# One of the first batch's loads in two halves, with a cast for each, and the instruction order written anew around it

## The chip, the core and the metric

The kernel runs on one core of a Trainium2 chip. A core has five engines that each follow their own queue in order: TensorE (PE, matrix products into PSUM), VectorE (DVE), ScalarE (ACT), GpSimd (POOL) and SyncE (SP, which here only starts DMAs). Semaphores tie the queues together. The metric is the time of one execution on the device in microseconds.

## What is computed

The inputs are q, k and v of 8 batches, 8 heads, 576 positions and 64 columns, and four weight matrices. All are float32.

```python
q_s = exp(q) / sum over the 64 columns          # per position
k_s = exp(k) / sum over the 576 positions       # per column
kv  = einsum('bhsd,bhse->bhde', k_s, v)         # 64x64 per head
x   = einsum('bhsd,bhde->bhse', q_s, kv)        # then (4608, 512): heads side by side
a, b = x @ w1, x @ w2                           # (4608, 1024) each
out = ((a * b) @ w3) @ w_out                    # (4608, 512)
```

The reference also takes the maximum off before each exponential, which cancels in the quotient.

## The kernel before

**Products of weights.** `w3 @ w_out` is one 1024x512 matrix, W3O. The kernel makes it once (lines 391 to 427): each of eight row blocks of w3 is loaded (`ld w3 n`, 512 KB), cast to 16 bits (`w3c`), transposed by TensorE (`w3t`, L406), copied out of PSUM (`w3e`), multiplied with the four cast pieces of w_out (`woc`; products `w3m`, L418) and copied out again (`w3v`).

**Attention.** For each batch b and each half i of the heads (lines 467 to 620): the exponentials of k (`ke`, ACT), a cast of v (`vc`), the exponentials of q (`qe`, ACT), row sums (`qr`, DVE), a reciprocal (`qi`), the normalisation (`qn`, L520), transposes (`qt`, on TensorE at L536 with copies `qv` for batches 0 to 3, by DMA for the others), then the products `kv` (L562), their division by the key sums (`kn`, DVE) and `x` (L607) with its copies to the tile xt (`xc`). The names in the lists below add batch, half and piece.

**Feed-forward.** The 4608 rows are taken in eight groups of 512 or 640. Group 0 is computed plainly (L647): `pa0`, `pa1` give x@w1 and `pb0`, `pb1` give x@w2, each product in two halves of the sum; `pac` copies the one out of PSUM and `pm` multiplies. The others use a Winograd scheme with seven products instead of eight on halves of the group (L712, tasks `x1` to `x4`, `w`, `v1`, `v2`): it needs combinations of the weights (`w1c`, `w2c` casts, `wc0` to `wc3`), combinations of xt (`tt1` to `tt4`), copies (`e1` to `e3`) and sums and products (`k1` to `k5`). Last, `s2` (L816) multiplies with W3O, `s2e` scales the result out of PSUM and `so` stores it.

**Buffers.** Every load lands in one of ten tiles `st`. A load into a tile that is in use waits, on SP's queue, until the reader of the old content is done, and everything behind it on that queue waits too. PSUM has eight tiles `ps`.

**The order.** No scheduler runs when the kernel is built. All steps are first recorded as numbered tasks. ORDER (line 18) lists the numbers in the order in which they are emitted, SLOTS (line 107) the tile of each buffer, and ENGS (line 139) the engine of each task that can run on several:

```python
for n in order:
    if isinstance(n, tuple):
        self.fill(self.pools[n[0]][n[1]], n[2])
    elif self.tasks[n].alts:
        self.tasks[n].emit(engs[n])
```

An entry `('ps', slot, n)` emits n matmuls on a blank tile (L985), which compute nothing that is used; here they are called fills.

Of the kernel before, what the change touches and what calls it, by code (L numbers as in the profile page):

```python
# [18 lines left out]
    ('ps', 0, 11), 12, 6, 0, 1, 2, 3, 14, 120, 96, 97, ('ps', 0, 3), 72, 98, 73, 121, ('ps', 0, 2), 74, 68,  # L19
    122, 75, 80, 99, 123, 8, 81, 4, 69, 5, 82, 76, 10, 124, 128, 9, 83, 7, 84, 129, 104, 100, 130, 13, 105,  # L20
    88, 11, 131, 106, 15, 89, 132, 70, 90, 107, 108, 16, 91, 112, 17, 77, 92, 19, 125, 144, 18, 113, 85,
    142, 114, 101, 143, 109, 115, 145, 133, 71, 20, 116, 146, 147, 117, 93, 78, 140, 21, 134, 126, 135, 86,
    127, 79, 110, 136, 94, 111, 137, 102, 95, 150, 152, 22, 162, 103, 148, 164, 118, ('ps', 3, 2), 151,
    154, 163, 138, 149, 153, 139, 168, 171, ('ps', 5, 8), 155, 169, 24, 170, 23, 156, 141, 87, 119, 25,
    172, 157, 173, 165, ('ps', 2, 2), 181, 166, 158, 180, 475, 159, 160, 167, 469, 161, 481, 174, 478, 176,
    175, 472, 182, 484, 466, 183, 487, 467, 26, 479, 468, 188, 488, 470, 473, 184, 471, 190, 485, 482, 486,
    476, 502, 189, 496, 185, 503, 474, 30, 490, 191, 504, 27, 480, 497, 28, 493, 477, 194, 491, 29, 489,
    508, 31, 492, 494, 483, 1382, 495, 1396, 202, 192, 499, 204, 1397, 203, 509, 498, 505, 200, 500, 205,
    511, 510, 501, 506, 214, 1403, 507, 512, 212, 206, 1404, 513, 207, 1389, 196, 215, 1390, 197, 1398,
    213, 1391, 40, 1405, 216, 34, 193, 1392, 217, 1383, 1393, 1399, 208, 1400, 1384, 201, 209, 199, 218,  # L30
    210, 219, 1385, 198, 186, 211, 32, 222, 177, 38, 223, 179, 178, 1386, 33, 220, 224, 1406, 221, 225, 36,
    1407, 226, 229, 232, 227, 230, 1408, 228, 235, 234, 231, 533, 233, 35, 237, 518, 236, 535, 1387, 519,
    563, 514, 534, 520, 37, 515, 548, 539, 42, 516, 549, 517, 522, 521, 564, 537, 552, 536, 538, 554, 523,
    553, 567, 540, 187, 525, 541, 524, 526, 555, 542, 578, 527, 528, 568, 545, 529, 556, 530, 570, 239,
    546, 593, 531, 558, 571, 547, 565, 557, 594, 569, 559, 573, 532, 579, 543, 244, 572, 560, 195, 544,
    597, 595, 574, 598, 575, 566, 246, 582, 550, 561, 608, 583, 596, 600, 623, 551, 601, 584, 576, 624,
    599, 562, 585, 256, 247, 1417, 577, 286, 627, 602, 1410, 245, 586, 242, 605, 609, 603, 240, 606, 1411,
    587, 588, 628, 607, 580, 604, 288, 612, 581, 630, 39, 625, 248, 631, 589, 590, 249, 1409, 613, 610,
    626, 629, 238, 591, 1418, 1388, 611, 614, 41, 615, 632, 1431, 43, 592, 616, 635, 241, 1395, 617, 633,
    618, 636, 254, 1394, 620, 634, 1432, 637, 280, 1402, 621, 1412, 243, 619, 1419, 1401, 622, 255, 1433,  # L40
    284, 252, 281, 257, 1434, 253, 1424, 258, 287, 250, 1435, 259, 1425, 298, 289, 1420, 296, 264, 251,
    265, 1421, 290, 1413, 283, 285, 266, 262, 267, 282, 260, 263, 1426, 291, 261, 44, 271, 268, 272, 273,
    306, 47, 270, 269, 277, 307, 45, 278, 1414, 297, 274, 657, 275, 279, 1427, 640, 308, 276, 294, 309,
    292, 658, 295, 672, 293, 644, 638, 642, 717, 639, 1428, 659, 299, 687, 641, 643, 661, 1430, 663, 673,
    660, 646, 662, 676, 48, 645, 647, 664, 300, 648, 1415, 677, 665, 649, 301, 702, 666, 650, 667, 49, 679,
    703, 668, 669, 1416, 680, 652, 651, 678, 670, 682, 52, 688, 654, 681, 706, 1437, 671, 655, 691, 718,
    302, 683, 707, 1423, 304, 656, 653, 692, 684, 721, 303, 305, 1429, 674, 685, 704, 694, 675, 722, 709,
    705, 693, 695, 686, 689, 724, 696, 732, 690, 725, 697, 699, 733, 698, 723, 708, 710, 700, 727, 711,
    1445, 701, 726, 736, 714, 728, 737, 712, 729, 715, 325, 738, 730, 739, 310, 713, 740, 1446, 716, 312,
    741, 734, 337, 719, 311, 742, 720, 747, 744, 735, 748, 749, 731, 745, 1438, 324, 743, 751, 753, 750,  # L50
    67, 752, 1439, 754, 1440, 755, 1441, 756, 757, 746, 1442, 759, 758, 316, 313, 1444, 317, 319, 314,
    1447, 760, 315, 1436, 320, 766, 321, 781, 318, 767, 1443, 1452, 328, 762, 796, 46, 811, 782, 763, 768,
    335, 761, 1453, 769, 770, 764, 1448, 771, 329, 783, 330, 785, 773, 765, 772, 55, 784, 774, 1454, 812,
    775, 776, 786, 1455, 331, 359, 787, 778, 1456, 1449, 815, 788, 777, 1450, 1466, 789, 779, 1459, 1422,
    797, 790, 816, 798, 780, 54, 800, 323, 332, 791, 799, 1451, 333, 793, 322, 792, 818, 1457, 826, 794,
    819, 1460, 336, 801, 817, 827, 1461, 820, 358, 1462, 795, 338, 821, 50, 803, 813, 334, 822, 804, 830,
    339, 802, 814, 831, 806, 340, 1463, 823, 1467, 805, 1468, 1464, 824, 841, 807, 833, 808, 825, 834,
    1469, 341, 809, 832, 842, 856, 810, 871, 835, 857, 858, 326, 836, 859, 843, 860, 837, 872, 838, 844,
    861, 327, 847, 875, 839, 845, 876, 1473, 846, 828, 1470, 848, 829, 863, 1472, 862, 849, 877, 864, 1465,
    878, 850, 851, 879, 865, 866, 1471, 853, 840, 881, 867, 868, 854, 342, 364, 880, 855, 343, 852, 366,  # L60
    873, 344, 363, 1474, 345, 53, 883, 869, 1475, 1458, 882, 346, 870, 352, 51, 347, 874, 1480, 348, 354,
    1481, 353, 1482, 884, 920, 886, 905, 921, 907, 885, 890, 906, 888, 922, 887, 891, 1483, 908, 1476, 889,
    1484, 894, 924, 1477, 1485, 895, 909, 935, 435, 925, 923, 892, 910, 59, 897, 893, 927, 898, 896, 936,
    912, 928, 362, 899, 926, 913, 911, 929, 900, 930, 914, 950, 60, 901, 902, 951, 915, 931, 939, 62, 917,
    916, 940, 1487, 56, 903, 942, 918, 1486, 904, 954, 943, 941, 955, 937, 944, 932, 373, 945, 938, 957,
    946, 1488, 958, 933, 1489, 365, 934, 952, 947, 367, 349, 355, 919, 1490, 350, 351, 356, 965, 948, 960,
    966, 1494, 953, 357, 995, 374, 969, 996, 1495, 371, 949, 1496, 368, 970, 956, 369, 57, 967, 361, 959,
    1497, 372, 1491, 999, 962, 972, 963, 1515, 973, 961, 980, 971, 968, 370, 981, 1516, 964, 1000, 974,
    975, 1498, 984, 375, 976, 1001, 376, 1002, 1479, 977, 1003, 1508, 978, 982, 1004, 1005, 985, 997, 409,
    1006, 1007, 987, 998, 360, 1501, 377, 1008, 986, 988, 1502, 983, 402, 1503, 1009, 989, 1478, 1504, 979,  # L70
    992, 1500, 1505, 990, 993, 378, 991, 1492, 379, 994, 1493, 1517, 381, 398, 1509, 380, 403, 1510, 382,
    391, 385, 384, 383, 1518, 393, 392, 386, 1014, 387, 1044, 407, 1010, 388, 1511, 389, 390, 66, 1015,
    1029, 1011, 58, 1016, 1030, 1046, 1013, 1017, 1045, 1031, 1018, 1519, 1032, 1059, 1033, 1019, 1035,
    1012, 1034, 1522, 1512, 1047, 1048, 1021, 1513, 1049, 1020, 1022, 1036, 1514, 1523, 1023, 1037, 1050,
    396, 1507, 1038, 1039, 1051, 1040, 64, 1041, 1052, 1524, 1521, 1042, 1060, 1054, 1043, 1026, 1520,
    1053, 1063, 1074, 65, 1055, 1064, 1089, 395, 1525, 408, 1061, 1075, 1066, 1062, 1024, 1067, 1078, 1027,
    1529, 1025, 1079, 1065, 1028, 1090, 1056, 1068, 400, 1069, 1530, 1057, 1526, 1071, 61, 1070, 1081, 394,
    401, 1527, 1093, 1080, 1094, 1091, 1072, 1076, 404, 1531, 1082, 1073, 1092, 1096, 1077, 1095, 405, 410,
    1097, 1104, 1532, 1105, 1083, 1119, 1533, 1098, 1099, 1084, 1120, 1108, 1085, 1101, 1058, 1109, 406,
    1123, 1102, 436, 1086, 1536, 1087, 1103, 1124, 1537, 1100, 399, 1506, 1111, 1088, 1126, 411, 1121,  # L80
    1112, 412, 397, 1550, 1122, 1110, 1127, 1114, 431, 1113, 1543, 1115, 1129, 430, 414, 437, 413, 415,
    1544, 433, 416, 1538, 417, 432, 1499, 1106, 1125, 434, 1107, 1116, 1528, 1551, 1128, 1535, 1552, 1117,
    1130, 1131, 1118, 418, 1132, 450, 419, 451, 1133, 420, 421, 452, 1545, 423, 438, 422, 1546, 453, 1136,
    1553, 1547, 439, 424, 1554, 1168, 425, 1138, 426, 1153, 1556, 1539, 440, 1154, 1134, 63, 1183, 1169,
# [167 lines left out]
def kernel(  # L252
# [11 lines left out]
    nc = tc.nc  # L264
# [754 lines left out]
```

## Time and profile before

| | us |
|---|---|
| median of 4 runs | 234.32 |
| the runs | 233.78, 233.90, 234.75, 235.75 |
| the profiled execution, its own time | 235.75 |
| its span, first to last instruction | 233.9 |
| TensorE busy in the span | 221.0 |
| VectorE busy | 187.7 |
| ScalarE busy | 140.7 |
| GpSimd busy | 91.6 |

The page gives shares of busy time, the span in 40 slices of 5.85 us (each digit is a share in tenths), and the chain of work that ended last. A line of the chain has a start, a length and what ran; "DMA st<-in_v_dram" is time waited for a transfer. In the timeline a line has start, length, engine, source line, operation, tiles written and read, and how often; in brackets stand the engine's idle time just before it and what ended that. L385 is a helper for all casts and copies, so its lines are told apart by their tiles. Matmuls overlap, so TensorE's busy time isn't the time at which it can follow: that is read from the distances between starts.

### The profile page before, as it was taken

The page shows a single profiled execution, that of the slowest core. Times are in us where ns is not written, and L with a number is a line of the kernel's source. Part 1 is how long each engine was busy: PE and PEld are TensorE (multiplying, and loading weights), DVE is VectorE, ACT ScalarE, POOL GpSimd, SP SyncE. Part 2 cuts the span into 40 slices and gives each one's busy share as a digit, 9 for nine tenths or more (in the row PEclk, how much of TensorE's full clock was granted, in tenths as well). Part 3 has the DMA queues.
Part 4 walks back from the last instruction along what each step waited for, and adds up shares of the span by engine and source line. Part 5 has one row for each costly group of instructions (what it writes and reads, how often), then busy time and mean ns, then how long its engine had stood idle before and what let it go on. Part 6 is the DMA issues. An engine that isn't in the chain of part 4 may idle for free.

```text
span 233.9 us, 5571 instructions
## 1 busy us (share of the span) xinstructions
PE 221.0 (94%) x2068; PEld 134.0 (57%) x2068; DVE 187.7 (80%) x457; ACT 140.7 (60%) x306; POOL 91.6 (39%) x81
## 2 busy tenths in 40 slices
PE   7759989998999999999999999999999999999991
PEld 2325444444676558866666676656665866566640
DVE  1322696899899998989998898899988998899930
ACT  2333692483889897768835847576898843525111
POOL 3113344819257787410383444530462503210300
PEclk9999999999999999999999999999999999999998
DMA  6989998788970959938895697859747763041535
GB/s 249 373 311 384 394 387 304 274 334 266 395 299 0 279 188 343 356 122 199 243 236 106 227 299 239 169 146 281 249 85 111 186 125 73 3 90 41 122 91 135
DMA packets 32732, 50.96 MB, mean 218 GB/s; under 512 B 11712, under 2 KB 11712, under 8 KB 32704
## 3 DMA queue, kind: packets, MB, share of 16 engines
q1 hardware_dynamic: 32304, 49.95, 69.5%
q10 hardware_dynamic: 400, 0.66, 1.2%
q8 instruction: 16, 0.26, 0.5%
q14 instruction: 12, 0.10, 0.1%
HBM read 38.80 MB, written 9.44 MB: 206 GB/s over the span
## 4 chain that ended last, share of the span: by engine, by line
PE 78%; DMA 9%; DVE 7%; POOL 2%; ACT 1%; issue 1%; SPq 1%; DVEq 0%; POOLq 0%
PE ps L712 41%; PE ps L816 22%; DMA st<-in_moe_w_dram 6%; PE ps L647 5%; PE ps L418 4%; DMA st<-in_v_dram 3%; PE ps L607 2%; PE ps L562 2%; DVE eq L520 1%; DVE ds L510 1%; DVE ab L664 1%; PE ps L536 1%; POOL eq L520 1%; SPq L332 1%; PE ps L406 1%
## 5 line engine op out<-in xcount | busy, mean ns | idle before, releaser
L736 DVE TENSOR_TENSOR cc<-ps,uu 128x320 f16<-128x320 f32 (+1 forms) x168 | 71.6, 454 | 7.4 <-PE ps L712 3.9
L816 PE MATMUL ps<-W3O,ab 128*128 128x512 f16 x288 | 77.3, 379 | 0.0
L385 ACT COPY uu<-ps 128x320 f32<-128x320 f32 (+1 forms) x144 | 54.1, 406 | 36.3 <-PE ps L712 25.7
L712 PE MATMUL ps<-tt,wc 128*128 128x320 f16 (+1 forms) x336 | 57.5, 288 | 0.1
L712 PEld LDWEIGHTS <-wc 128*128 128x128 f16 x448 | 43.5, 98 | 19.7 <-issue 0.5
L520 POOL TENSOR_TENSOR eq<-eq,ds 128x1152 f16<-128x1152 f16 x14 | 30.0, 2145 | 35.5 <-DVE ds L517 26.9
L712 PEld LDWEIGHTS <-w 128*128 128x128 f16 x336 | 32.1, 98 | 16.6 <-issue 0.8
L712 PE MATMUL ps<-xt,w 128*128 128x320 f16 (+1 forms) x224 | 39.7, 288 | 0.0
L763 POOL TENSOR_TENSOR ab<-cc,cc 128x320 f16<-128x320 f16 (+1 forms) x27 | 20.0, 751 | 47.9 <-DVE cc L736 47.8
L816 PEld LDWEIGHTS <-ab 128*128 128x128 f16 x288 | 27.0, 98 | 18.5 <-issue 0.7
L736 DVE TENSOR_TENSOR ab<-ps,cc 128x320 f16<-128x320 f32 (+1 forms) x56 | 25.1, 454 | 1.4 <-PE ps L712 0.2
L789 ACT ACTIVATE osb<-ps 128x512 f32<-128x512 f32 x29 | 17.2, 602 | 13.9 <-PE ps L816 13.8
L385 ACT CAST xt<-ps 128x512 f16<-128x512 f32 (+3 forms) x43 | 15.0, 408 | 13.8 <-PE ps L607 13.8
L510 DVE TENSOR_REDUCE ds<-eq 128x9 f32<-128x576 f16 x32 | 23.2, 741 | 0.0
L506 ACT ACTIVATE eq<-st 128x576 f16<-128x576 f32 x32 | 21.3, 686 | 2.3 <-DMA st<-in_q_dram 1.8
L712 PE MATMUL ps<-tt,w 128*128 128x320 f16 (+1 forms) x112 | 22.6, 288 | 0.0
L712 PE MATMUL ps<-xt,wc 128*128 128x320 f16 (+1 forms) x112 | 22.3, 288 | 0.0
L475 ACT ACTIVATE ek<-st 128x576 f16<-128x576 f32 x32 | 21.1, 685 | 0.6 <-ACT ek L475 0.6
L689 POOL TENSOR_TENSOR tt<-xt,tt 128x640 f16<-128x640 f16 (+1 forms) x6 | 7.8, 1294 | 22.9 <-DVE tt L689 14.4
L418 PE MATMUL ps<-ab,ab 128*128 128x512 f16 x64 | 15.0, 379 | 0.3 <-DVE ab L385 0.3
L647 PE MATMUL ps<-xt,w 128*128 128x512 f16 x64 | 14.9, 379 | 0.0
L385 POOL CAST v<-st 128x1152 f16<-128x1152 f32 x11 | 13.0, 1193 | 4.3 <-DMA st<-in_v_dram 4.3
(55 smaller groups left out, 199.8 us busy)
## 6 DMA issues: line engine op xcount, KB each, us to landing
st<-in_q_dram SPq DMA_DIRECT2D x16, 576.0 KB, 5.6
st<-in_v_dram SPq DMA_DIRECT2D x16, 576.0 KB, 6.6
st<-in_k_dram SPq DMA_DIRECT2D x16, 576.0 KB, 5.8
out_dram<-osb SPq DMA_DIRECT2D x67, 128.0 KB, 2.6
st<-in_moe_w_dram SPq DMA_DIRECT2D x16, 512.0 KB, 8.5
st<-in_moe_w_out_dram SPq DMA_DIRECT2D x4, 512.0 KB, 7.9
out_dram<-osb ACTq DMA_DIRECT2D x5, 128.0 KB, 2.6
qsT<-eq SPq DMA_TRANSPOSE x8, 3.4
```

The source lines that it names most:

```text
L385: {"DVE": nc.vector.tensor_copy, "POOL": nc.gpsimd.tensor_copy, "ACT": nc.scalar.copy}[eng](out=o, in_=i)
L418: nc.tensor.matmul(pp.tile, lhsT=wT.tile[:, gt * P:(gt + 1) * P], rhs=wo[i][1].tile[:, (gt % 2) * C:(gt % 2 + 1) * C], start=(gt == 0), st ...
L475: nc.scalar.activation(out=ek.tile[:, :, j, :], func=AF.Exp, in_=vk(bk.tile)[:, j].rearrange("p (r d) -> p r d", r=RK))
L506: nc.scalar.activation(out=eq.tile[:, :, j, :], func=AF.Exp, in_=vq(bq.tile)[:, j].rearrange("p (r d) -> p r d", r=RK))
L510: nc.vector.tensor_reduce(out=ds.tile[:, 0, j], axis=AX.X, op=ALU.add, in_=eq.tile[:, :, j, :])
L520: {"POOL": nc.gpsimd, "DVE": nc.vector}[e].tensor_tensor(out=eq.tile, in0=eq.tile, op=ALU.mult, in1=ds.tile[:, 1].rearrange("p j r -> p r ...
L647: nc.tensor.matmul(ps.tile[:, 0:m], lhsT=w[qt][:, ct, fo:fo + P], rhs=x[:, ct, lo:lo + m], start=(ct == 0), stop=(ct == 3))
L712: nc.tensor.matmul(ps.tile[:, 0:h], lhsT=lhs(c), rhs=rhs(c), start=first and c == 0, stop=c == 1, skip_group_check=not first)
L736: return lambda: nc.vector.tensor_tensor(out=dst(), in0=ps.tile[:, 0:h], in1=other.tile[:, 0:h], op=op)
L763: {"POOL": nc.gpsimd, "DVE": nc.vector}[e].tensor_tensor(out=ab.tile[:, 0:h], in0=c11.tile[:, 0:h], in1=c21.tile[:, 0:h], op=ALU.mult)
L789: nc.scalar.activation(out=o(), in_=i(), func=AF.Copy, scale=ISC)
L816: nc.tensor.matmul(po.tile[:, :w], lhsT=rows(ab_buf[(g, ft)].tile), rhs=W3O[:, ft, m * w:(m + 1) * w], start=(ft == 0), stop=(ft == N_FT - 1))
```

## The change

The load of v for batch 0, second half of the heads, becomes two transfers of 288 KB into the two halves of one tile, and its cast becomes two casts of 576 elements per partition, one for each transfer:

```diff
-    JB = []
+    JB = [('v', 0, 1)]
+    XTAIL = []
...
-        if b in JB:
+        if (x, b, i) in JB:
             bb = buf("st")
...
-            if b in JB:
+            if ("v", b, i) in JB:
                 vs = []
                 for j in range(2):
                     def c_j(e, v16=v16, bv=bv, vv=vv, j=j):
                         cast(e, v16.tile[:, :, j, 0:D], vv(bv.tile)[:, j].rearrange("p (r d) -> p r d", r=RK))
                     vs.append(add("POOL", ("vc", b, i, j), c_j, [tv[j]], [bv, v16],
                                   dict(POOL="copy", ACT="sb", DVE="cast"), n=576))
...
+            if b in XTAIL:
+                pieces = [(0, 8)]
```

XTAIL is empty, so nothing of its branch is emitted. The tables ORDER, SLOTS and ENGS are replaced as a whole, so nearly every step stands at another place than before. TensorE's real matmuls are the same in number and shape.

The loads on SP's queue up to the last weight, each with the `st` tile that it lands in:

```text
before: w3 6 [9], w3 3 [0], w3 0 [7], wo 0 [3], w3 1 [1], wo 1 [2], w3 7 [6], w3 4 [1], w3 2 [5], wo 2 [8],
        w3 5 [9], q 0 0 [3], wo 3 [0], v 0 0 [1], k 0 0 [7], q 0 1 [4], k 0 1 [8], v 0 1 [2], then w12 x8
after:  w3 5 [7], w3 3 [4], w3 1 [6], w3 0 [0], w3 6 [3], wo 0 [5], wo 1 [7], w3 7 [8], wo 2 [1], w3 4 [2],
        wo 3 [4], w3 2 [0], q 0 0 [5], q 0 1 [6], k 0 0 [9], v 0 0 [8], w12 x2 [7, 3], k 0 1 [2],
        v 0 1 second half [5], first half [5], w12 x2 [0, 7], w12 [5], w12 x3 [8, 6, 7]
```

What the other engines do first:

```text
ACT  before: woc 0, w3e 6, w3e 1, w3e 7, w3e 2, qe 0 0, woc 3, vc 0 0, w3v 6, ke 0 0, qe 0 1, w3v 3, qe, ke 0 1
     after:  w3c 1, w3c 3, w3e 6, w3c 4, w3e 4, qe 0 0, w3v 7, ke 0 0, w3v 3, w3v 1, qe 0 1, xc 0 0, w2c 0 0, xc 0 0 8, ke 0 1
DVE  before: w3c 3, w3e 3, w3e 0, w3c 1, woc 1, w3c 7, w3c 2, w3e 4, w3e 5, qr 0 0, qi, w3v x4
     after:  w3c 5, w3c 6, w3e 1, w3e 3, w3e 5, w3e 0, woc 1, w3e 7, woc 3, qr 0 0, qi, w3e 2, w3v x3
POOL before: w3c 6, w3c 0, w3c 4, woc 2, w3c 5, qn 0 0, vc 0 1, w1c, w1c, wc0, w2c, wc2, qn 1 0, vc 1 1, wc2
     after:  w3c 0, woc 0, w3c 7, woc 2, w3c 2, qn 0 0, vc 0 0, w1c, qn 0 1, vc 0 1 (second half), wc2, w2c, w1c,
             wc0, wc3, wc1, qn 1 1, vc 1 1
PE   before: fill x11, w3t 3, fill x3, w3t 0, w3t 6, fill x2, w3m 0, ... fills x2, x8, x2 around the first x
     after:  fill x17, w3t 3, w3t 1, w3t 5, w3t 0, w3t 6, fill x3, w3m 1, ... fill x4 after the first x
```

In the new order DVE casts the first half of v 0 1 after two W3O copies and one xt copy.

The number of tasks on each engine that changes, over the whole kernel:

| task | before | after |
|---|---|---|
| fill matmuls | 28 | 24 |
| k5 on DVE, on POOL | 29, 27 | 20, 36 |
| e1, e2, e3 on ACT, on DVE | 144, 24 | 138, 30 |
| tt1 to tt4 on DVE, on POOL | 21, 7 | 16, 12 |
| wc0 to wc3 on DVE, on POOL | 4, 4 | 2, 6 |
| qv on ACT, on DVE | 4, 12 | 9, 7 |
| qn on DVE, on POOL | 2, 14 | 3, 13 |
| pac on ACT, on DVE | 4, 4 | 6, 2 |
| s2e on ACT, on DVE | 29, 7 | 32, 4 |
| w3c on DVE, ACT, POOL | 4, 0, 4 | 2, 3, 3 |
| w3e on DVE, ACT | 4, 4 | 6, 2 |
| xc on ACT, on DVE | 43, 21 | 42, 22 |
| stores issued by SP, by ACT | 67, 5 | 65, 7 |

## The prediction

> **What bounds the kernel now.** I read the page's shares and slices first, then the chain of waits that ended last, then the timeline of the first 40 us.
>
> ```profile
> PE 221.0 (94%) x2068; PEld 134.0 (57%) x2068; DVE 187.7 (80%) x457; ACT 140.7 (60%) x306; POOL 91.6 (39%) x81
> PE   7759989998999999999999999999999999999991
> PEclk9999999999999999999999999999999999999998
> ```
>
> TensorE is full from slice 5 on; the holes are at the start. From the chain (start, length, what):
>
> ```profile
> 2.61 7.99 DMA st<-in_moe_w_dram
> 10.62 0.70 DVE ab L385
> 11.34 5.36 DMA st<-in_moe_w_dram
> 16.76 1.05 POOL ab L385
> ...
> 22.85 6.47 PE ps L418 x30
> ...
> 54.78 2.22 DVE eq L520
> 57.13 0.66 PE ps L536 x9
> ...
> 61.16 10.78 PE ps L712 x78
> ...
> 77.35 7.22 DMA st<-in_v_dram
> 84.69 1.14 POOL v L385
> 85.84 2.11 POOL eq L520
> ...
> 229.10 0.60 ACT osb L789
> ```
>
> Until 17 us weight loads set the pace, then TensorE, with short stops at 57 and 86. L418 x30 in 6.47 us is 0.216 us per 512-column matmul; the 320- and 256-column ones of L712 follow each other at 0.136 and 0.109, transposes at 0.056. With these, all TensorE work without the fills is 206.2 us: 416 x 0.216 + 448 x 0.136 + 336 x 0.109 = 187, the rest transposes, kv and x. I place times by how much of it is done. When `pa1 0 0` starts at 39.55, 23.2 are done: 16.3 lost. At the first Winograd matmul (61.09) 43.0: another 1.7. From there to the end of the last matmul (229) 4.6, then 5.0 of tail. 206.2 + 16.3 + 1.7 + 4.6 + 5.0 is the 233.9 span. Only these losses can change, since the change keeps every real matmul.
>
> Why the 16.3:
>
> ```profile
> 1.19 4.87 PE L985 MATMUL ps<-blank 128*128 128x512 f16 x11 [1.19 <-DVE blank L978]
> 3.72 8.43 SPq L332 DMA_DIRECT2D st<-in_moe_w_dram  x3
> 6.72 0.81 PE L985 MATMUL ps<-blank 128*128 128x512 f16 x3
> 16.76 1.04 POOL L385 CAST ab<-st 128x1024 f16<-128x1024 f32 x1 [7.70 <-DMA st<-in_moe_w_dram]
> 31.14 1.15 POOL L385 CAST v<-st 128x1152 f16<-128x1152 f32 x1 [3.54 <-DMA st<-in_v_dram]
> ```
>
> The SP queue stands for seven us (second line): the eighth load, w3 4, needs the buffer of w3 1, whose cast ends at 11.31. Its data lands at 16.7, 3.5 us after the seventh's 13.2, where busy queues land one every 1.31 (512 KB) or 1.5 us (576 KB). So 2.2 us of transfer time are lost.
>
> **The change, part by part.** *Load order.* Landings by place, from before: 4.1, 5.4, 8.0, 9.3, 10.6, 11.9, 13.2. In the new order the first wait is for the cast of w3 5 (lands 4.1, DVE 0.69: 4.8); the next, wo 3, waits for w3 3, cast on ACT behind w3 1 (8.0 + 2 x 1.05 = 10.0). Six loads are still in flight or queued then, so the queue doesn't dry up: 14.5, 15.8, 17.1, 18.4, 19.7 for the twelve weights (before: 23.6), q at 21.2 and 22.7, k 24.2, v 25.7, two w12 at 27.1 and 28.4, k 29.9, the halved v 31.4, w12 at 32.8 and 34.1.
>
> *W3O.* `w3t 3` can start at 10.05, `w3t 6` after DVE's cast of the fifth load (11.3), four PSUM copies follow on DVE (0.69 each, to 13.9), POOL casts wo 0 by 13.0: the first product at 13.05 (before 10.5). Behind it data is ahead: wo 2's cast is ready at 16.9 and wanted at 17.8, w3 4's 18.2 and 20.0, w3 2's 20.8 and 21.3. TensorE is dense from 13.05, and the last product ends at 29.2 (before 30.8).
>
> *Batch 0.* The first q is in at 21.2; two exponentials (0.68 each, behind an ACT copy to 22.0) end at 23.3, two sums on DVE (0.74) at 24.1, the reciprocal at 24.4, the normalisation on POOL (2.15) at 26.65, and its transposes stand among W3O products, so TensorE doesn't wait. v's cast follows on POOL (1.19, to 27.85), kv at 27.9, the division of both halves on DVE (0.4 each, behind two qsT copies) to 29.3, x at 29.35 (before 31.6). ACT then still owes two W3O copies (0.59) and the second q's exponentials; xt (two of 0.59) is out at 30.9 and w2's cast (1.05) at 32.0; three pb0 pairs (0.43 each) run to 33.3, with about 1.0 of waiting ahead of them. The second q's sums end at 30.7 on DVE, POOL normalises it by 33.2, its transposes end at 34.1, kv at 34.5, division at 35.4, x after it; four pa0/pb0 pairs carry TensorE to 37.5, where the 23.2 are done: **2.05 us earlier**. A POOL cast of w1 at 27.85 that takes 2.05, as at 33.84 before, instead of 1.04 still ends at 29.9, ahead of xt. The split itself: v's cast was 1.15-1.19 in one piece; two halves in parallel are about 0.6 on POOL (33.2 to 33.8) and 0.69 on DVE. It saves 0.5 only if the cast is last; here the transposes end later, so I take 0, bounds -0.5 to +0.4 (one more issue: SP's are 0.37 to 0.45). The DVE half has `kn 0 1`, an xt copy and wc behind it; its data is two us old. The slot passes to the next w12 load when both casts are done (34.0), with all later loads queued behind on SP: it lands at 37.6 (3.6 for a load on an empty queue, as q 1 0's), cast on ACT by 38.9, where the copies of pa1 wait from 39.3: 0.4 of cover, beyond it each us is a us.
>
> *To the Winograd stage.* 19.8 of work. Before lost 0.88 waiting for a normalisation of 2.2 on DVE and 0.8 in x. The new order puts that one on POOL and another on DVE, moves wc0 and wc1 of the second half and wc3 of the first to POOL, and leaves DVE 16 us of work where it had 18. The kn and xt copies remain: after the last kv two s2 pairs (0.87) cover some 1.5. I take 1.4 lost (bounds 0.8 to 2.5), **0.3 gained**.
>
> Here a rule is weighed. Before, a wc combination on POOL took 2.13 beside a light DVE, 2.57 and 3.23 beside a busy one. The Trainium skill, GPSIMD Engine Reference, section Engine selection, says not to put two-input elementwise work on GpSimd (about twice the time), which speaks against the moves. POOL's row is wc2, w2's cast, w1's cast, wc0, wc3, wc1, qn, vc: at 2.13 each it ends at 52.5, and kv 1 1 wants it at 55.8; by 3.23 each, with casts at 2.05 as once in this trace, it ends near 56.7 and w2's cast comes 1.6 late for pb1. So 0 by the low row, 1.7 by the high one; I take 0.2 (most rows lie low).
>
> *Body.* Nine k5 products go from DVE (0.28-0.34) to POOL (0.67-0.79), six of e1 to e3 go from ACT to DVE, tt sums go to POOL; DVE's total falls by 4, ACT rises by 4.6, POOL by 13, all far under TensorE's 206. Before lost 4.6 us there, mostly in x and at 86. The late v 3 1 of 77.35 came of an SP queue that waited at 63-75; the new order issues it earlier: up to 1.0 gained. As other places may stop in turn, I take 0, bounds -1.2 to +2. The tail is the same scaled copy and store: 0.
>
> *Fills.* 28 become 24; their time is in the losses already. Seventeen stand first. Eleven took 4.87 at 0.43 each, later ones 0.216, while PEclk says full: the row does not show this start-up rate. Twelve at 0.43 and five at 0.216 end near 7.6; `w3t 3` comes at 10.05, so they hide in 2.4 us of waiting. But the next real matmul (fill x3) comes at 12.3; between lie only 40 transposes. The Trainium skill, TensorE: Matmul & The Clock Gate, section What's actually happening, says the clock falls to half after about 3.4 us idle, and its section Part 4: PE-mode transpose says transposes don't count as busy. The longest such stretch before, 15.46 to 18.31 with one transpose group, was followed by pairs at the full 0.43. By that row nothing is lost; by the rule, 4.7 us without matmuls, 3.4 us of dense work run at half speed: 1.7. The row is shorter than the case, so both stay; I take 0, as 2.2 of the 4.7 are streaming transposes.
>
> Empty XTAIL runs nothing. Sum: 2.05 + 0.3 - 0.2 = 2.15. The profiled execution took 235.75, 1.85 outside its span; its sum is 233.6. It was the slowest of four runs; from their median 234.32: **232.2**.
>
> **The rivals.** A measurement here tells about 1% (2.3 us) from no change.
> - *Clock falls in the first 13 us.* For it: the rule and the 4.7 us. Against it: full rate after 2.85. It takes 1.3-1.7 of the gain: 233.7.
> - *POOL is the bound at 34-56.* For it: 3.23 and 2.05 beside a busy DVE. Against: POOL idles long before. Gain 0.5: 233.8.
> - *Slower: the products moved to POOL end late for s2.* Nine more k5 (a Winograd product that s2 reads), each 0.45 longer and in one queue with qn (2.15). All exposed cost 4.1, and 1.9 remain after the gain of 2.15: 236.2. It decides from five exposed. Against it: with 27 on POOL, L816's loads stood 0.2 us in all for POOL.
> - *More than predicted.* The body also loses its stop at 86 and the DVE has slack: 230.6.
> - *The split does nothing by itself.* Then the new order does it all, and the time is the forecast's.
>
> **How the numbers follow.** Forecast 0.40 (232.2 +- 0.8 from the 0.5 to 1.1 of its open costs; faster by over 1% begins at 232.0, so 0.18 of it lies beyond), clock 0.22, POOL 0.12, slower 0.16 (0.13 beyond 1%, at 236.7, where stops that my sums can't see come to it; else within), more 0.10, all beyond. Two hundredths of clock and POOL also end beyond, if the body gives its 1.0. Faster by over 1% 0.30, within 0.57, slower 0.13. The range reaches from the middle of the last case to just under the slower one's centre, and leaves out about 0.05 below and 0.13 above: 230.5 to 235.8.
>
> **What would show it.** Right: the w3 casts wait nowhere over 2 us after 8 us; the last W3O product at about 29; 32 pairs of L647 beginning their second halves near 37.5; the first L712 near 59; no L816 waiting for POOL. Wrong: L418 spaced 0.43 instead of 0.216 after 13 us (clock); pb1 waiting for POOL's cast of w2; new holes in the middle slices of PE, or L712 waiting for uu or tt, which my sums of work can't see.

## The result, and the profile after

| | before | after |
|---|---|---|
| median, us | 234.53 (58 runs) | 233.59 (37 runs) |
| lowest and highest, us | 233.0 to 239.05 | 231.88 to 235.93 |
| the profiled execution, us | 235.75 | 233.48 |
| its span, us | 233.9 | 231.7 |

The ratio is 0.9959, with an interval of 0.9944 to 0.9974. The change makes the kernel faster by 0.41%: 0.95 us of 234.53, between 0.6 and 1.3. The prediction was 232.2 us, 2.1 less than the median it started from. The direction was right and the size was more than twice what came. The two profiled executions are 2.27 us apart, though, almost the 2.15 of the sum. Ratios and their intervals leave out the few executions that lie over 1.5% above the fastest of their kernel; among them are one of before and one of a kernel below that took 458 and 457 us, for which no trace was kept.

In the profile after, the source lines stand a little lower, because the diff adds lines: W3O's products are L419 (L418 before), group 0 is L675 (L647), Winograd L740 (L712), casts L386 (L385), s2 L844 (L816), fills L1013 (L985). These are two rows of its 40 slices of 5.8 us each.

```profile
PE   7699979899999999999999999999999999999991
PEclk9999999999999999999999999999999999999999
```

The third slice, 5 before, is now a 9: the hole at 12 to 17 us is closed. The sixth and the eighth, 8 and 9 before, are now 7 and 8: longer stops there than before had. Next the SP queue of after (start, length, what it starts).

```profile
0.74 2.44 SPq L333 DMA_DIRECT2D st<-in_moe_w_dram  x5
...
8.85 0.37 SPq L333 DMA_DIRECT2D st<-in_moe_w_out_dram  x1
9.31 0.41 SPq L333 DMA_DIRECT2D st<-in_moe_w_dram  x1
11.85 0.88 SPq L333 DMA_DIRECT2D st<-in_q_dram  x2
```

The standing of seven us is gone (the waits for the first casts are now 1.9 us before 8.85 and 2.1 before 11.85): all twelve weights have been asked for by 9.7 us, and the first q follows at 11.85. The last weight lands at 18.63 (23.55 before). Then the chain of work that ended last, in after.

```profile
3.22 7.50 DMA st<-in_moe_w_out_dram
10.73 0.05 issue
10.78 1.05 POOL ab L386
11.85 9.77 DMA st<-in_q_dram
...
32.78 0.68 POOL v L386
33.47 0.37 SPq L333
33.84 0.05 issue
33.89 6.65 DMA st<-in_moe_w_dram
40.54 0.05 issue
40.59 1.05 POOL w L386
41.64 0.05 issue
41.69 6.23 PE ps L675 x28
...
58.57 3.48 PE ps L740 x24
```

The run of L418 from 22.85 has left the chain. What stands there now is the first half batch's attention up to POOL's half of the new cast (`POOL v`, ending 33.46). SP waits for that cast, then asks for a w12 load; the next one behind it lands at 40.54, 6.65 us after it was issued, and TensorE waits for its cast on POOL until 41.69. The timeline of TensorE in after has that wait in brackets:

```profile
35.35 5.34 PE L675 MATMUL ps<-xt,w 128*128 128x512 f16 x24
41.69 6.22 PE L675 MATMUL ps<-xt,w 128*128 128x512 f16 x28 [1.00 <-POOL w L386]
```

This stop of 1.00 us, called the stop at 41 below, was not in the prediction.

### The profile page after: what moved, and what is told of

Its sections match the earlier page's. It is cut to its first block, busy times and chain, and to the rows that moved or that the text cites. A ratio compares the mean times of both kernels' runs of the same rounds, so it can differ in the third digit from the quotient of the medians.

```text
span 231.7 us, 5587 instructions
## 1 busy us (share of the span) xinstructions
PE 220.2 (95%) x2064; PEld 133.7 (58%) x2064; DVE 180.7 (78%) x440; ACT 142.3 (61%) x310; POOL 101.8 (44%) x95
## 4 chain that ended last, share of the span: by engine, by line
PE 70%; DMA 16%; DVE 7%; POOL 2%; issue 1%; SPq 1%; ACT 1%; DVEq 0%; POOLq 0%
PE ps L740 40%; PE ps L844 22%; DMA st<-in_q_dram 7%; DMA st<-in_moe_w_out_dram 3%; DMA st<-in_moe_w_dram 3%; PE ps L675 3%; PE ps L610 3%; DVE ds L511 2%; DMA qsT<-eq 2%; PE ps L563 2%; PE ps L537 1%; SPq L333 1%; DVE eq L521 1%; DVE ab L692 1%; DVE W3O L386 1%
## 5 line engine op out<-in xcount | busy, mean ns | idle before, releaser
L844 PE MATMUL ps<-W3O,ab 128*128 128x512 f16 x288 | 76.1, 379 | 0.0
L386 ACT COPY uu<-ps 128x320 f32<-128x320 f32 (+1 forms) x138 | 51.4, 411 | 25.4 <-PE ps L740 17.5
L740 PE MATMUL ps<-tt,wc 128*128 128x320 f16 (+1 forms) x336 | 57.6, 288 | 0.5 <-ACT uu L386 0.5
L740 PEld LDWEIGHTS <-wc 128*128 128x128 f16 x448 | 43.0, 98 | 20.6 <-issue 1.4
L791 POOL TENSOR_TENSOR ab<-cc,cc 128x256 f16<-128x256 f16 (+1 forms) x36 | 25.5, 718 | 63.6 <-DVE cc L764 58.9
L740 PE MATMUL ps<-xt,w 128*128 128x320 f16 (+1 forms) x224 | 41.7, 288 | 0.0
L740 PEld LDWEIGHTS <-w 128*128 128x128 f16 x336 | 32.3, 98 | 15.8 <-issue 0.7
L844 PEld LDWEIGHTS <-ab 128*128 128x128 f16 x288 | 27.0, 98 | 19.9 <-issue 0.9
L521 POOL TENSOR_TENSOR eq<-eq,ds 128x1152 f16<-128x1152 f16 x13 | 27.9, 2146 | 11.9 <-DVE ds L518 10.3
L817 ACT ACTIVATE osb<-ps 128x512 f32<-128x512 f32 x32 | 19.2, 606 | 17.9 <-PE ps L844 17.9
L386 ACT CAST xt<-ps 128x256 f16<-128x256 f32 (+3 forms) x42 | 13.8, 393 | 13.0 <-PE ps L610 12.8
L740 PE MATMUL ps<-xt,wc 128*128 128x320 f16 (+1 forms) x112 | 21.8, 288 | 0.0
L740 PE MATMUL ps<-tt,w 128*128 128x320 f16 (+1 forms) x112 | 21.8, 288 | 0.0
L675 PE MATMUL ps<-xt,w 128*128 128x512 f16 x64 | 14.6, 379 | 1.6 <-POOL w L386 1.0
L419 PE MATMUL ps<-ab,ab 128*128 128x512 f16 x64 | 15.0, 379 | 0.1
L386 DVE CAST xt<-ps 128x512 f16<-128x512 f32 (+3 forms) x22 | 10.3, 497 | 4.7 <-PE ps L610 4.7
L386 DVE COPY uu<-ps 128x320 f32<-128x320 f32 (+1 forms) x30 | 13.3, 453 | 0.3
```

Source lines behind the costliest of these rows:

```text
L386: {"DVE": nc.vector.tensor_copy, "POOL": nc.gpsimd.tensor_copy, "ACT": nc.scalar.copy}[eng](out=o, in_=i)
L419: nc.tensor.matmul(pp.tile, lhsT=wT.tile[:, gt * P:(gt + 1) * P], rhs=wo[i][1].tile[:, (gt % 2) * C:(gt % 2 + 1) * C], start=(gt == 0), st ...
L521: {"POOL": nc.gpsimd, "DVE": nc.vector}[e].tensor_tensor(out=eq.tile, in0=eq.tile, op=ALU.mult, in1=ds.tile[:, 1].rearrange("p j r -> p r ...
L675: nc.tensor.matmul(ps.tile[:, 0:m], lhsT=w[qt][:, ct, fo:fo + P], rhs=x[:, ct, lo:lo + m], start=(ct == 0), stop=(ct == 3))
L740: nc.tensor.matmul(ps.tile[:, 0:h], lhsT=lhs(c), rhs=rhs(c), start=first and c == 0, stop=c == 1, skip_group_check=not first)
L791: {"POOL": nc.gpsimd, "DVE": nc.vector}[e].tensor_tensor(out=ab.tile[:, 0:h], in0=c11.tile[:, 0:h], in1=c21.tile[:, 0:h], op=ALU.mult)
```

## The experiments

*Theory A*: the profiled execution that the forecast was summed against was a slow one of its kernel, its front above all, so the change removes less from a typical execution than from that one. *The rival*: that front is the kernel's own, and the new order gives half of the gain back, by the stop at 41 or by the split. The runs show that the first is most of it, and that the second is there too, in part of the executions.

Each execution is placed by four times of its trace: the landing of the third load on SP's queue, the end of the last W3O product, the start of the ninth group 0 pair (`pa1 0 0` with its work of 23.2 us done, which the prediction placed at 37.5), and the first Winograd matmul (predicted near 59).

**Before, unchanged, a second time.**

> The kernel before, unchanged, profiled a second time. The forecast was summed against one execution (span 233.9, 16.3 us lost up to 39.55). Theory A (that execution was a slow one of its kernel, and the gain was added up against its losses): this profile has a span near 232.8, with the missing us found in a stage that the change shortens. Theory B (the profile was typical, the gain of 2.2 in the traces is lost in the other executions of the new kernel): span 233.5 to 234, the start of the first Winograd matmul again at 61.1. Time against before: ratio 1.000.

Measured: median 234.6 us, ratio 0.998 (0.995 to 1.001), the profiled execution 233.0 with a span of 231.2. Its chain of work that ended last begins so:

```profile
2.61 6.77 DMA st<-in_moe_w_dram
9.41 0.70 DVE ab L385
10.13 3.47 DMA st<-in_moe_w_dram
13.65 1.05 POOL ab L385
...
58.10 3.95 PE ps L712 x27
```

The same chain is in the prediction with 7.99, 0.70, 5.36 and 1.05, and with the first Winograd matmul at 61.16 in place of 58.10. The same kernel started its Winograd stage three us earlier because the first loads came sooner: 1.22 us in the first line and 1.89 in the third. So a front of before isn't one number. Two more executions:

> The kernel before, unchanged, a third execution under the profiler. So far its first Winograd matmul stood at 61.09 us in one execution and at 58.04 in another. If the execution that the forecast was summed against was a late one of a spread (theory A), this one lies anywhere from 58 to 61 and follows the landing of the third load: landing by 6.8 goes with a first Winograd matmul at 58.0 to 58.7, landing near 8.0 with 60 to 61. If the early execution was the exception (rival), it is at 60.5 to 61.5 with the load at 8.0.

> The kernel before once more, a fourth execution under the profiler, expected as the third: theory A says that over the four the first Winograd matmul averages 59.3 to 60.1 us, and that the third load's landing sorts them; the rival says that three of four are at 60.5 or later.

They took 233.98 and 236.04 us. All four together (us):

| before | third load lands | w3 4 issued, lands | last W3O product ends | ninth pair | first Winograd matmul | its time |
|---|---|---|---|---|---|---|
| the profile of the prediction | 7.96 | 11.34, 16.71 | 30.77 | 39.55 | 61.09 | 235.75 |
| second | 6.75 | 10.13, 13.60 | 27.80 | 36.49 | 58.04 | 233.0 |
| third | 7.41 | 10.81, 14.72 | 29.13 | 37.83 | 59.37 | 233.98 |
| fourth | 7.98 | 11.36, 15.29 | 29.86 | 38.56 | 60.11 | 236.04 |

The mean of the last milestone is 59.65, inside what theory A expected; the rival wanted three of four at 60.5 or later, and there is one. The third load sorts them but for the two latest, where it differs by 0.02 only. What it brings late goes down the chain of before: w3 1 lands behind it, its cast frees the tile, and w3 4 can only then be asked for. The execution behind the prediction had that and also the slowest landing of w3 4 itself, 5.36 us where the others had 3.5 to 3.9. It was the latest of the four at the ninth pair, by 1.44 us against their mean. In time the fourth is the longest: from the first Winograd matmul to the last matmul it took 169.25 us, the others 167.9 to 168.3.

**After, unchanged, again.**

> The changed kernel, unchanged, profiled a second time. Theory A: span near 231.7 again, first Winograd matmul at 58.5, ratio 0.996. Theory B: the profile on record was a lucky one, this one has a span near 232.5 with a new stop in the front or the first W3O products at half rate.

Measured: median 233.82, ratio 0.9973 (0.9948 to 0.9998); the first Winograd matmul at 58.60, where the first profile has 58.54. Four more executions followed later (their expectation is about the clock, which is taken up below):

> The kernel after, unchanged, a third execution under the profiler. In 11 of 38 timed executions its granted clock averages 0.989 to 0.993 and these take about 1.5 us more than the others. If the clock rival of the prediction is what they are, an execution of that kind shows a clock below 1 in the first 17 us, with the products of W3O 0.43 us apart instead of 0.216; if it is the 1.2 us stop at 40 us, it shows there, with L675 at 0.43 after it; otherwise somewhere in the body. An execution of the other kind shows none and its first Winograd matmul at 58.4 to 59.0.

> As the third look at the kernel after: first Winograd matmul at 58.4 to 59.0 us where the clock is full up to there, and a clock below 1 in one place, to be named, where the mean is 0.993 or less.

> As the fourth look. By the share of 11 in 38, one or two of these four looks fall to the kind with the lower clock.

> As the fifth look. If none of the four falls to that kind, where its clock drops stays open.

| after | third load lands | last weight lands | last W3O product ends | ninth pair | w12 behind the stop lands | first Winograd matmul | its time |
|---|---|---|---|---|---|---|---|
| the profile above | 6.81 | 18.63 | 28.96 | 37.08 | 40.54 | 58.54 | 233.48 |
| second | 6.99 | 18.82 | 28.92 | 37.05 | 40.60 | 58.60 | 233.75 |
| third | 7.38 | 19.20 | 28.79 | 36.91 | 40.48 | 58.48 | 233.25 |
| fourth | 7.51 | 19.32 | 28.91 | 37.03 | 40.89 | 58.89 | 233.75 |
| fifth | 7.63 | 19.47 | 29.12 | 37.25 | 42.12 | 60.11 | 234.99 |
| sixth | 6.83 | 18.67 | 28.79 | 36.92 | 40.39 | 58.39 | 233.46 |

The third load still varies, by 0.8 us, and the last weight with it. The end of W3O varies by 0.33 and does not follow. In the new order SP's longest wait for a cast of those first loads is 2.1 to 2.7 us, with six loads still under way, so the lateness stays in slack. But the stop at 41 has its own spread: in the fifth execution the w12 load lands at 42.12, TensorE stands for 2.40 us, and all of it is in the time. None of the four fell to the kind with a mean clock of 0.993 or less, so where its clock drops stays open. The third execution has a mean of 0.994, and its clock is full up to the last matmul (226.4 us); it falls only in the tail (0.69 between 227 and 231 us), which costs nothing. The same holds for the traces below that are called full in clock. Of 38 executions of after, the profiled one among them, 11 have a mean clock of 0.993 or less, with medians of 234.73 (0.992 or less, eight of them) and 234.39 (0.993, three) against 233.15 for the other 27; of before, eight of 44 are at 0.9945 or less, and only the two at 0.992 or less stand out (236.6 against 234.6).

**The split alone, in the old order.** Order, tiles and engines of before; the load in two transfers one after the other, both casts on POOL.

```diff
-    JB = []
+    JB = [('v', 0, 1)]
```

> The order of before with the load in two transfers and both casts on POOL, one after the other. The cast is not what kv 0 1 waits for in the old order (it is at 32.3, kv at 33.8), so every theory of mine expects 1.000 within 0.002; if halving a load costs transfer time for all that is queued behind it, 1.002 to 1.004.

Measured: 234.81 us, ratio 1.0014 (0.9979 to 1.0049). Its third load landed at 8.03 and its first Winograd matmul came at 59.84, between the third and the fourth execution of before. Alone, the split is worth nothing that this can measure: a gain of 0.5 us at most by the interval. So the gain is not the split's by itself.

**The first wait alone.** One number of the tile list of before: w3 4 lands in a tile that is free (4) and doesn't wait for the cast of w3 1. All else is as before.

```diff
-    7, 3, 1, 2, 5, 8, 0, 0, 1, 3, 9, 7, 9, 1, 6, 4, 8, 2, 6, 9, 5, 0, 7, 1, 8, 4, 0, 3, 9, 4, 1, 5, 5, 2,
+    7, 3, 1, 2, 5, 8, 0, 0, 4, 3, 9, 7, 9, 1, 6, 4, 8, 2, 6, 9, 5, 0, 7, 1, 8, 4, 0, 3, 9, 4, 1, 5, 5, 2,
```

> The order of before, with one number changed: w3 4 lands in tile 4, which is free until the load of q 0 1, instead of tile 1 with w3 1 in it. It takes the first wait of SP's queue away and nothing else. Theory A (the change gains because its early loads wait for no cast, and the old front is slow in the executions where that wait is long): the twelve weights are in by 20 to 21, the first Winograd matmul starts near 58.5, ratio 0.995 (0.993 to 0.997), as much as the change. Rival (the gain comes of the moved DVE and ACT work): weights earlier, but 0.998 to 1.000.

Measured: 233.26 us, ratio 0.9962 (0.9938 to 0.9986); two of its twelve executions, at a mean clock of 0.991 and 0.992, took 236.9 and are not in the ratio. Its SP queue:

```profile
3.62 2.00 SPq L332 DMA_DIRECT2D st<-in_moe_w_dram  x3
5.66 0.61 SPq L332 DMA_DIRECT2D st<-in_moe_w_out_dram  x1
8.03 0.33 SPq L332 DMA_DIRECT2D st<-in_moe_w_dram  x1
```

The x3 that took 8.43 us before takes 2.00. The third load was late in this execution too (7.95), but w3 4 lands at 14.47, right behind w3 7's 13.19; the weights are in by 21.22, and Winograd starts at 58.83. One number in the tile list gives as much as the whole change (0.9962 against 0.9959). This shows the mechanism of the prediction's first part and its worth, about one us (0.3 to 1.5 by the interval).

**The new order with the load whole.** The change without its split: one transfer of 576 KB, one cast on POOL at the place of POOL's half. The numbers in ORDER and ENGS shift with the two tasks that go; the sequence on every engine is otherwise that of after.

```diff
-    JB = [('v', 0, 1)]
+    JB = []
```

> The new order with the load of v 0 1 in one transfer and one cast on POOL, at the place of POOL's half. If the split does nothing by itself: ratio 0.996 as with it. If the split carries part of the gain: the cast ends 0.5 later on POOL (its 1.15 for 0.67), and the tile passes on 0.1 earlier or later, so 0.998 at most; if DVE's half costs more than it gives, 0.994.

Measured: 236.29 us (234.9 to 237.31), ratio 1.0063 (1.0028 to 1.0099). The expectation missed: slower than before, and 2.5 us slower than after in the runs beside it (233.82). Here the split matters. The cast of v on POOL takes 1.14 instead of 0.67 and ends at 33.84; the w12 load that waits for the tile is asked for 0.4 later, and the one behind it lands at 42.20. Not all of this is the split's doing: that load comes 4.67 behind the first one here, and with the halves it came 4.76 behind in the fifth execution of after and 2.99 to 3.41 in the other five. TensorE in this kernel, first by the timeline, then in stretches (us, TensorE's busy time, granted clock, DMA share, GB/s):

```profile
35.74 5.34 PE L675 MATMUL ps<-xt,w 128*128 128x512 f16 x24
43.35 6.82 PE L675 MATMUL ps<-xt,w 128*128 128x512 f16 x23 [2.27 <-POOL w L386]
```

```profile
35.70:41.20 5.50, 5.34 (x24) 1.00 0.87 257
41.20:43.30 2.10, 0.00 (x0) 1.00 1.02 394
43.30:44.80 1.50, 1.45 (x5) 0.72 0.77 222
44.80:46.30 1.50, 1.50 (x5) 0.50 0.80 293
46.30:47.80 1.50, 1.50 (x6) 0.64 1.05 406
47.80:50.00 2.20, 2.20 (x12) 1.00 1.03 391
```

After the stop the granted clock is 0.72, 0.50 and 0.64 in three stretches of 1.5 us. That is as much as 3.4 us at half speed ((0.28 + 0.50 + 0.36) x 1.5 x 2), an estimated cost of 1.7. The last group 0 pair starts at 52.39 and Winograd at 61.89. A second execution:

> The order of the change with the last load whole, a second execution under the profiler. If the 2.4 us stop at its first pa0 0 6 is what brings the half rate (0.43 us a matmul for some 3.5 us), the same stretch is in this execution as well, and its last L647 pair starts at 52 to 53 us. If that stretch was one execution's own, the matmuls follow at 0.216 and the pair starts near 50.6, and then the whole load's loss against the change's own time is the longer stop alone, 1.3 us.

It took 235.04 us, with a shorter stop and a full clock:

```profile
36.14 5.34 PE L675 MATMUL ps<-xt,w 128*128 128x512 f16 x24
42.68 6.22 PE L675 MATMUL ps<-xt,w 128*128 128x512 f16 x28 [1.20 <-POOL w L386]
```

The load landed at 41.53 in place of 42.20, so this did not repeat the long stop and can't say what always follows one. The last pair started at 50.03. The timed executions of this kernel fall in two groups: 237.15, 237.29 and 237.31 us at a mean clock of 0.991 or 0.992, and 234.9, 235.19 and 235.43 at 0.995 or more.

**The stop filled.** The same, with ten fills just ahead of the matmul that stops:

```diff
-    489, 502, 30, 511, 190, 29, 505, 468, 508, 28, 509, 477, 31, 191, 496, 34, 471, 490, 36, 510, 503, 192,
+    489, ('ps', 7, 10), 502, 30, 511, 190, 29, 505, 468, 508, 28, 509, 477, 31, 191, 496, 34, 471, 490, 36,
```

> The new order with the load of v 0 1 whole (ratio 1.006 when looked at before), and ten fills on the free PSUM tile 7 ahead of pa0 0 6, where TensorE stood still for 2.43 us and then ran eight matmuls at 0.43 us each. If that half rate is the clock falling for want of matmuls: the eight follow at 0.216, 1.7 us come back, ratio 0.999. If it is something else (operands late, PSUM): still 0.43, 1.006.

> The same with the ten fills in that stop, a second execution under the profiler. If fills keep the rate, no stretch of 0.43 follows the stop, and the last L647 pair starts at 50.3 to 51.0 us; if the half rate comes by execution and not by the stop, it can show here as well and the pair starts at 52 or later.

Measured: 235.44 us (234.79 to 238.22), ratio 1.0054 (1.0022 to 1.0087). In both profiled executions the matmuls follow at full rate behind the fills; the second one's timeline (L1013 are the fills):

```profile
40.98 2.32 PE L1013 MATMUL ps<-blank 128*128 128x512 f16 x10
43.14 6.21 PE L675 MATMUL ps<-xt,w 128*128 128x512 f16 x28
```

The fills also outlast the wait. In the same execution the cast that TensorE waits for ends at 42.30, 0.84 before the matmuls start (in the other, at 42.73 and 0.90):

```profile
41.26 1.04 POOL L386 CAST w<-st 128x1024 f16<-128x1024 f32 x1 [4.30 <-DMA st<-in_moe_w_dram]
```

The last pair starts at 50.97 and 50.48. Eleven of the twelve timed executions have a clock of 0.993 or more; one has 0.990 and took 238.22. Against 0.999, which was expected if the clock were the whole loss, the ratio is a miss. The fills take away most of the slow group of the kernel without them, and cost up to 0.9 us themselves. What is left shows in the three profiled executions at full clock, the one without fills among them: Winograd starts at 59.52, 60.48 and 59.98, by 0.7, 1.6 and 1.1 us later than the mean of after (58.84). Without the 0.9 and 0.8 by which the fills outlast the wait, that is 0.3 to 0.7, from the later cast and load. So the clock was the loss of half the executions, and the late load is a loss of all, but a small one: at full clock the whole load takes 235.19 (the median of the three timed executions above), 1.4 more than the five executions of after at 0.997 or more in the same runs (233.75), and its front explains half of that at most.

**A free tile for the load that stops.** One number of the tile list of after, so that the w12 load which waited for the tile of v 0 1 (5) lands in one that is free (1).

```diff
-    0, 5, 6, 7, 0, 1, 4, 4, 2, 5, 7, 9, 3, 8, 8, 6, 2, 5, 7, 3, 0, 7, 8, 5, 6, 7, 8, 3, 4, 9, 1, 6, 5, 9,
+    0, 5, 6, 7, 0, 1, 4, 4, 2, 5, 7, 9, 3, 8, 8, 6, 2, 5, 7, 3, 0, 7, 8, 1, 6, 7, 8, 3, 4, 9, 1, 6, 5, 9,
```

> The changed kernel, with one number changed: the first w12 load of the second half lands in tile 1, free since 15.8, instead of tile 5, which it shares with the halved v. Theory: the stop of 1.16 us before pa0 0 6 is that wait, passed on by SP's queue; it goes, and the ratio is 0.991 to 0.992. If the stop comes of the transfers themselves (they landed 3.1 us apart where 1.3 is usual): it stays, 0.996.

Measured: 232.07 us, ratio 0.990 (0.9871 to 0.9929), faster than both kernels. The load is issued at 29.19 instead of 33.47, the one behind it lands at 37.99 instead of 40.54, and TensorE runs through:

```profile
35.52 11.38 PE L675 MATMUL ps<-xt,w 128*128 128x512 f16 x52
46.74 1.03 PE L844 MATMUL ps<-W3O,ab 128*128 128x512 f16 x4
```

52 matmuls stand in one line where after had 24, a stop and 28. Winograd starts at 57.54, 1.0 earlier than in the first profile of after. This shows that the stop was the wait for that tile. The same free tile with the load whole:

```diff
-    JB = [('v', 0, 1)]
+    JB = []
...
-    0, 5, 6, 7, 0, 1, 4, 4, 2, 5, 7, 9, 3, 8, 8, 6, 2, 5, 7, 3, 0, 7, 8, 5, 6, 7, 8, 3, 4, 9, 1, 6, 5, 9,
+    0, 5, 6, 7, 0, 1, 4, 4, 2, 5, 7, 9, 3, 8, 8, 6, 2, 5, 7, 3, 0, 7, 8, 1, 6, 7, 8, 3, 4, 9, 1, 6, 5, 9,
```

> The load whole, and the free tile for the w12 load as in the other kernel of this call. Theory: the split mattered only because the tile passes on later without it, and the stop then grew past what the clock bears. With the tile free the split is worth only its later cast, 0.4 us on kv 0 1: ratio 0.992 to 0.994. If the split is worth more by itself: 0.997 and over.

Measured: 232.77 us, ratio 0.9942 (0.991 to 0.9974); Winograd at 57.56, as with the halves. So part of what the split is worth in this order is that it passes the tile on 0.4 us sooner to a load that TensorE waits for; where nobody waits for the tile, the front is the same with it and without it. That is not all. The intervals of the two ratios overlap, but the executions hardly do: with the halves eight of the ten in the ratio took 231.21 to 232.19, with the whole load all twelve took 232.51 or more, and the medians of these are 231.83 and 232.77. In the two traces the whole load falls 0.7 us behind between the first Winograd matmul and the last one. 0.3 of it comes near 98 us, where a `tt` sum on POOL waits for a TensorE product instead of one of DVE's, here with the halves and then with the whole load:

```profile
97.58 1.40 POOL L717 TENSOR_TENSOR tt<-xt 128x640 f16<-128x640 f16 x1 [2.62 <-DVE cc L764]
97.88 1.39 POOL L717 TENSOR_TENSOR tt<-xt 128x640 f16<-128x640 f16 x1 [2.96 <-PE ps L740]
```

It is so in all five traces with the whole load and in none of the seven of this order with the halves; why isn't shown. The rest comes at 168 to 176 us and near 200, where executions of one kernel differ as much.

## Why the prediction was wrong in size

The step that failed is the first term of the sum, "When `pa1 0 0` starts at 39.55, 23.2 are done: 16.3 lost", and what was made of it at the end: "It was the slowest of four runs; from their median 234.32: **232.2**". The 16.3 was taken from one execution as if each had it. Over four executions the ninth pair starts at 39.55, 36.49, 37.83 and 38.56, a mean of 38.11: 14.9 lost, 1.44 less. The new order removes the loss that varies. So the excess of that one execution over its kernel's median, 235.75 - 234.32 = 1.43 us, was part of the 2.15 to be gained, and it may not be subtracted from the median as well. (That 1.43 and 1.44 are so near is chance; against the mean time of the four profiled executions, 234.69, the excess is 1.06.) The prediction had the other number in the line before: "its sum is 233.6". The kernel after takes 233.59. That it fits to 0.01 is luck: the ninth pair came 0.46 earlier than forecast (37.04 for 37.5), and the stretch from there to Winograd took 0.36 longer (21.80 for 21.44).

By the means of four executions of before and six of after:

| stretch | forecast | measured |
|---|---|---|
| to the ninth pair | 2.05 | 38.11 - 37.04 = 1.07 |
| from there to the first Winograd matmul | 0.3 - 0.2 | 21.54 - 21.80 = -0.26 |
| from there to the last matmul | 0 | 168.35 - 168.23 = 0.1 |
| sum | 2.15 | 0.9 |

The timed gain is 0.95. Point by point:

- *Load order, W3O, batch 0: right in time.* Forecast for after were the last W3O product at 29.2 and the ninth pair at 37.5; they are at 28.79 to 29.12 and at 36.91 to 37.25. The first product came at 11.87 in the first profile of after, not at 13.05, because wo 0 landed at 10.73 where the landings of before had 11.9 for its place: the third load again. The end did not move with it. That this part works through SP's first wait is shown by the kernel that takes only that wait away.
- *To the Winograd stage: the stop at 41.* The prediction put the waiting w12 load at 37.6, and it landed at 37.42. It gave 0.4 of cover and said that each us beyond it is a us. The load that mattered was the next one, which it did not place: on a queue that follows at 1.31 it would have come at 38.7, and it came at 40.54. That is a stop of 1.0 to 1.4 in five executions of six, and of 2.4 in the other. The 1.4 that was taken as lost in this stretch came near by luck only: the loss measured is 2.0 (21.80 less the 19.8 of work), but with the free tile, where the stop is gone, the stretch takes 20.29. So the copies of kn and xt, to which the 1.4 was put down, cost about 0.5, and the stop 1.5.
- *The split itself, "I take 0, bounds -0.5 to +0.4", and the rival "does nothing by itself".* True in the old order; false in the new order as it stands, where the medians are 2.5 us apart (236.29 and 233.82), and with the free tile, where they are 0.9 apart though the front is the same. The cast was looked at for who reads v, while in the front what counted was who gets its tile.
- *Clock falls in the first 13 us: not seen.* In six profiled executions of after the granted clock is full up to 20 us, and L419 runs x14 in 3.18 us from 11.87, 0.216 apart, though before the three fills ahead of it there were 3.5 to 5.2 us with nothing on TensorE but 40 transposes. Whether transposes count as work for the clock isn't shown by that. A fall was caught only in another kernel, after the stop with the whole load. What slows the 11 of 38 executions with a lower mean clock was not caught; their 1.2 to 1.6 us over the others is about the size of the 1.7 of that one fall. So part of the missing gain, 0.44 us between the medians of all executions and of those at full clock, has no place yet.
- *POOL as bound: did not come.* The two-input products on POOL took 2.11 to 2.13 us in after's timeline of POOL, none of them the 2.57 or 3.23 of before, and no stop of TensorE from 42 us to Winograd that ends on POOL is over 0.5 us:

```profile
44.76 2.11 POOL L437 TENSOR_TENSOR wc<-w 128x1024 f16<-128x1024 f16 x1 [3.13 <-ACT w L386]
46.83 2.13 POOL L437 TENSOR_TENSOR wc<-w,wc 128x1024 f16<-128x1024 f16 x1
48.91 2.13 POOL L437 TENSOR_TENSOR wc<-wc,w 128x1024 f16<-128x1024 f16 x1
```

- *Slower through k5 on POOL: did not come.* TensorE's s2 matmuls waited 0.2 us in all for POOL (a single wait), with 36 of the products there, as with 27.
- *Body and tail 0: right*, 0.1 and nothing.

## What to carry to other kernels

A term that a change removes has to be sized from more than one execution when it hangs on when the first loads land; with one at hand, forecast the new kernel's absolute time from it (here 233.6 for 233.59, the last tenths by luck) and don't carry the difference over to a median that the profiled execution lies above. In a ring of landing tiles, ask of every cast who gets the tile next and who waits for that load and for those behind it on the queue: here one free tile gave as much as the whole new order (0.9962 against 0.9959), and another one in the new order took it to 0.990. And fills put into a wait should end before the wait does: ten of them here cost up to 0.9 us.

## What the runs showed of the hardware

**The third load.** It lands at 6.70 to 8.03 us in the executions above, whatever the kernel, while the first two, where the trace has them, land at 4.1 to 4.3 and 5.3 to 5.6 us. Those behind it keep their distance of 1.3. No run here tells why.

**A queue that has run dry.** In after the DMAs move next to nothing between 32.4 and 34.8 us, while SP waits for the casts of v. The rate in 40 slices of 0.4 us from 30 to 46 us:

```profile
GB/s 381 403 376 390 384 210 36 26 26 61 0 41 195 312 358 287 159 26 184 261 302 246 379 410 394 210 230 333 338 303 403 412 399 398 415 409 392 277 225 346
```

The first load into the dry queue lands 3.95 us after its issue, and the next, issued 0.42 later, 3.12 behind it instead of 1.3 (4.76 in the fifth execution of after), with the rate back at about 390 only near 39. Why the second is so late isn't shown. With the free tile, asked for 4.3 earlier, the second lands 1.25 behind the first.

**The clock after a stop.** TensorE stood idle for 2.27 us in the kernel with the whole load and then ran about 3.4 us at half speed; it stood for 2.40 us in the fifth execution of after and then ran at full speed at once:

```profile
43.27 6.22 PE L675 MATMUL ps<-xt,w 128*128 128x512 f16 x28 [2.40 <-POOL w L386]
```

From the first matmul after the stop to the last group 0 pair it is 9.04 us in the one and 7.35 in the other: 1.69 between two stops of equal length. The Trainium skill, TensorE: Matmul & The Clock Gate, section What's actually happening, puts the fall after about 3.4 us of idling and says that the window in which this is counted runs freely. The measured stretch at half speed has that length; the fall came after less idling than the page says. That the window's phase decides which stop is punished would fit both executions, but no run here measures it.
